# Turning results back twelve products after their last one, also across the border of batches

## The chip, the cores and the metric

The kernel runs on one core of one Trainium2 chip. The metric is device time in microseconds (us) of one execution; the figures given are the median of a few runs. TensorE (PE in the profile) multiplies and transposes, VectorE (DVE) and ScalarE (ACT) work on tiles and read the matmul results, GpSimd (POOL) works on tiles in main on-chip memory, and SyncE (SP) issues most of the transfers. Each engine has a queue of its own and runs it in the order in which the program lists the work; they meet through semaphores.

## The reference

For 8 batches, 8 heads, a sequence of 576 and a head size of 64, attention that keeps the 32 largest scores of each row, then a low-rank mixer over the sequence and a two-layer network over the channels:

```python
scores = scale * np.matmul(q, k.transpose(0, 1, 3, 2))
kth = np.partition(scores, -top_k, axis=-1)[..., -top_k:-top_k + 1]
scores = np.where(scores >= kth, scores, -1000000000.0)
attn = softmax(scores)                     # with + 1e-09 in the denominator
x = heads_to_channels(np.matmul(attn, v))  # (8, 576, 512)
xt = x.transpose(0, 2, 1)
u = x + (xt @ U @ V).transpose(0, 2, 1)    # rank 32
ch = np.maximum(u @ w_ch1, 0.0) @ w_ch2    # 512 -> 2048 -> 512
return (u + ch).astype(np.float32)
```

## The kernel before

Attention runs in 160 steps: 32 pairs of heads (four pairs to a batch), five row tiles to a pair. The main loop (from L788) lists, for each step, work on several tiles at once: score products for the next tile (`scores`, L323) with ScalarE copies out of PSUM (L351, L340), the search for the 32nd largest value on VectorE and GpSimd (`fold`, `split`, `front`), exponentials on ScalarE (L397), and the turning of the weights so that they can be multiplied with V. In the later pairs most of that turning is shared: VectorE transposes 32 x 32 blocks (`blocks`, L518), SyncE writes them to a scratch tensor in DRAM (L524), and ScalarE issues the transfer that brings them back as PT (`back`, L533); a last strip is transposed by TensorE (`turns`, L557) and copied by ScalarE (L558). `values` multiplies PT with V (L587, L591; L577 for the fifth tile). When a pair is done, `mixed` turns its result (L614, L618), divides by the sums of the weights on GpSimd (L619), and makes the pair's part of u, transposed (L625, L633, L637, L639, L647).

The two-layer network of a batch is `mlp(b)`, a generator of single products. It is put on the list `fillers` when the batch's last pair is mixed, and `fill()`, called some nine times in a step, draws products from it by a running balance `due`, so that they are spread between the attention work on TensorE's queue. The 576 columns of u are done in two parts, 320 and 256 wide. For each part there are 16 blocks of the hidden layer, of four products each (L662) and a Relu on ScalarE (L674), and then four blocks of results, c = 0 to 3, of sixteen products each (L681). A block of results is copied from PSUM by ScalarE (L696), and GpSimd adds u (L697); in the last batch VectorE does both in one (L694). The matmul results lie in two PSUM buffers (`ps_m`, two deep), and the hidden layer in ten pairs of tiles.

The result tile oT is still transposed. The function `turned_back` makes a job for it: TensorE transposes it in two or three pieces (L729) into a PSUM buffer of `ps_t`, two deep and shared with `turns`, `values` and `mixed`; ScalarE copies it to ob (L731, and L733 for the last 64 rows, which belong to the first part); SyncE writes it out (L735, L740). In the last batch the job is a VectorE transpose (L711) with transfers from it (L716, L721), but for its very last result. The job isn't run at once, but kept in the list `late`:

```python
if f == 4 and late:        # after the Relu of hidden block 4: 20 products on
    late.pop()()
...
if f == 12 and late:       # in the next block of results: 13 products on
    late.pop()()
...
late.append(turned_back(b, chunks, lo, c, oT))
...
late.pop()()               # end of mlp(b): the last result of the batch, at once
```

So the results c = 0, 1, 2 are turned back after 13 more products, the result c = 3 of the first part after 20, and the last one of the batch directly after its own addition.

Of the kernel before, what the change touches and what calls it, by code (L numbers as in the profile page):

```python
# [26 lines left out]
def kernel(  # L27
# [98 lines left out]
    def rows(t):  # L126
        return P if t < NT else TAIL
# [475 lines left out]
    def mixed(g, wait, lag=0):  # L603
# [45 lines left out]
        if gi == NPAIR - 1:  # L649
            fillers.append(mlp(b))  # L650

    def mlp(b):

        uT = uTs.pop(b)
        late = []
        for chunks, (lo, hi) in zip(PARTS, SPAN):
            w = hi - lo
            hTs = []
            for f in range(NF):
                ph = ps_m.tile([P, C], F32, tag="mm", name="mm")  # L660
                for cc in range(NC):
                    nc.tensor.matmul(  # L662
                        ph[:, 0:w],
                        lhsT=w1[:, cc, f * P : (f + 1) * P],
                        rhs=uT[:, cc, lo:hi],
                        start=(cc == 0),
                        stop=(cc == NC - 1),
                    )
                    if cc < NC - 1:
                        yield w / C  # L670
                if f % 2 == 0:
                    hT = mlpp.tile([P, 2, WIDE], F32, tag="hT", name="hT", bufs=HT)
                    hTs += [hT[:, 0], hT[:, 1]]
                nc.scalar.activation(hTs[f][:, 0:w], ph[:, 0:w], AF.Relu)  # L674
                if f == 4 and late:
                    late.pop()()
                yield w / C
            for c in range(NC):
                po = ps_m.tile([P, C], F32, tag="mm", name="mm")
                for f in range(NF):  # L680
                    nc.tensor.matmul(  # L681
                        po[:, 0:w],
                        lhsT=w2[:, f, c * P : (c + 1) * P],
                        rhs=hTs[f][:, 0:w],
                        start=(f == 0),
                        stop=(f == NF - 1),
                    )
                    if f == 12 and late:
                        late.pop()()
                    if f < NF - 1:  # L690
                        yield w / C
                oT = mlpp.tile([P, WIDE], F32, tag="oT", name="oT")
                if b == B - 1:
                    nc.vector.tensor_tensor(oT[:, 0:w], uT[:, c, lo:hi], po[:, 0:w], ALU.add)  # L694
                else:
                    nc.scalar.copy(oT[:, 0:w], po[:, 0:w])  # L696
                    nc.gpsimd.tensor_tensor(oT[:, 0:w], oT[:, 0:w], uT[:, c, lo:hi], ALU.add)  # L697
                late.append(turned_back(b, chunks, lo, c, oT))
                yield w / C
        late.pop()()  # L700

    def turned_back(b, chunks, lo, c, oT):


        def run():
            cs = slice(c * P, (c + 1) * P)
            if b == B - 1 and (lo, c) != (SPAN[1][0], NC - 1):

                w = sum(rows(t) for t in chunks)
                ob = mlpp.tile([P, 3 * P], F32, tag="ob", name="ob", bufs=2)  # L710
                nc.vector.transpose(ob[:, 0:w], oT[:, 0:w])  # L711
                for a in range(4):
                    cs = slice(c * P + a * BLK, c * P + (a + 1) * BLK)
                    ba = ob[a * BLK : (a + 1) * BLK]
                    for t in chunks[0:2]:
                        nc.sync.dma_start(  # L716
                            out[b, 0:MAIN, cs].rearrange("(m i t) c -> t i m c", i=BLK, t=NT)[t],
                            ba[:, OFF[t] - lo : OFF[t] - lo + P].rearrange("i (m c) -> i m c", c=BLK),
                        )
                    if NT in chunks:  # L720
                        nc.sync.dma_start(  # L721
                            out[b, MAIN:S, cs].rearrange("(m i) c -> i m c", i=BLK),
                            ba[:, 2 * P : 2 * P + TAIL].rearrange("i (m c) -> i m c", c=BLK),
                        )
                return
            tp = ps_t.tile([P, 3, P], F32, tag="tp", name="tp")
            for i, t in enumerate(chunks):
                n = rows(t)
                nc.tensor.transpose(tp[0:n, i, :], oT[:, OFF[t] - lo : OFF[t] - lo + n], ident)  # L729
            ob = mlpp.tile([P, 3, P], F32, tag="ob", name="ob", bufs=2)  # L730
            nc.scalar.copy(ob[:, 0:2], tp[:, 0:2, :])  # L731
            if NT in chunks:
                nc.scalar.copy(ob[0:TAIL, 2], tp[0:TAIL, 2, :])  # L733
            t = chunks[0]
            nc.sync.dma_start(  # L735
                out[b, 0:MAIN, cs].rearrange("(p t) c -> p t c", t=NT)[:, t : t + 2, :],
                ob[:, 0:2],
            )
            if NT in chunks:
                nc.sync.dma_start(out[b, MAIN:S, cs], ob[0:TAIL, 2])  # L740

        return run
# [11 lines left out]
    def fill(k=1):  # L754


        nonlocal due
        for _ in range(k):
            if passes:
                passes.pop(0)()  # L760
            if mixing and next(mixing[0], True):
                mixing.pop(0)
            due += share * (SHORT if t == NT else 1) * (EARLY if n <= 2 * ALONE + 2 else 1)
            while due > 0:
                if not fillers:
                    due = 0.0
                    break
                done = next(fillers[0], None)
                if done is None:
                    fillers.pop(0)  # L770
                else:
                    due -= done
# [132 lines left out]
        fill(2)  # L905
    while mixing or fillers:
        fill()


# [29 lines left out]
```

## Time and profile before

| what | value |
|---|---|
| median of 3 runs | 1717.11 us (1716.77 to 1718.14) |
| profiled execution, own time | 1716.93 us |
| its span, first to last instruction | 1715.1 us |
| TensorE matmul busy | 1612.5 us (94%) |
| VectorE busy | 1485.3 us (87%) |
| ScalarE busy | 1023.3 us (60%) |
| GpSimd busy | 944.3 us (55%) |
| mean granted TensorE clock | 0.970 |

In the profile, a line such as "L729 PE MATMUL" is work of line 729 of the kernel on TensorE; "out<-in" names the tile that is written and those that are read. "PE x <- POOL y" in a list of waits means that TensorE stood before x until GpSimd had done y. PEld is TensorE's loading of weights, which overlaps its matmuls. A product in float32 shows as two matmul records. Ends of matmuls are modelled, and some records may be missing. The attention ends at about 1555 us, and from about 1587 us on only the last batch's network is left, 128 us long. Batches 2 to 5 repeat with a period of 193.8 us.

### The profile page before, as it was taken

The page shows a single profiled execution, that of the slowest core. Times are in us where ns is not written, and L with a number is a line of the kernel's source. Part 1 is how long each engine was busy: PE and PEld are TensorE (multiplying, and loading weights), DVE is VectorE, ACT ScalarE, POOL GpSimd, SP SyncE. Part 2 cuts the span into 40 slices and gives each one's busy share as a digit, 9 for nine tenths or more (in the row PEclk, how much of TensorE's full clock was granted, in tenths as well). Part 3 has the DMA queues.
Part 4 walks back from the last instruction along what each step waited for, and adds up shares of the span by engine and source line. Part 5 has one row for each costly group of instructions (what it writes and reads, how often), then busy time and mean ns, then how long its engine had stood idle before and what let it go on. Part 6 is the DMA issues. An engine that isn't in the chain of part 4 may idle for free.

```text
span 1715.1 us, 29634 instructions
## 1 busy us (share of the span) xinstructions
PE 1612.5 (94%) x9489; PEld 1218.3 (71%) x9489; DVE 1485.3 (87%) x4317; ACT 1023.3 (60%) x2582; POOL 944.3 (55%) x749
## 2 busy tenths in 40 slices
PE   4566799998999999999999999999999999999999
PEld 2444566787777877788677877788677877788777
DVE  7999989999999999999999999999999999992000
ACT  4888797665656556565656566565655566563100
POOL 4778578656555555565555555565555555552000
PEclk7678899999999999999999999999999999999999
DMA  3322322344444444444444444444444444432010
GB/s 86 95 84 84 84 75 62 79 113 124 117 112 118 115 112 106 116 112 118 111 112 115 115 110 107 115 105 122 112 111 119 116 109 102 114 93 71 4 16 13
DMA packets 275837, 167.37 MB, mean 98 GB/s; under 512 B 173920, under 2 KB 260192, under 8 KB 275680
## 3 DMA queue, kind: packets, MB, share of 16 engines
q1 hardware_dynamic: 259648, 110.67, 27.5%
q10 hardware_dynamic: 16032, 54.79, 9.9%
q8 instruction: 75, 1.23, 0.3%
q14 instruction: 82, 0.67, 0.1%
HBM read 101.42 MB, written 63.96 MB: 96 GB/s over the span
## 4 chain that ended last, share of the span: by engine, by line
PE 68%; DVE 25%; DMA 2%; issue 2%; POOL 2%; ACT 1%; SPq 1%; DVEq 0%; POOLq 0%; ACTq 0%
PE mm L662 25%; PE mm L681 21%; DVE upper L458 8%; DVE m L463 7%; PE sc L323 7%; PE O L591 5%; DVE first L446 3%; DVE y L518 1%; PE tp L557 1%; PE O L577 1%; PE up L637 1%; PE O L587 1%; DVE lower L434 1%; DVE upper L436 1%; DVE upper L432 1%
## 5 line engine op out<-in xcount | busy, mean ns | idle before, releaser
L681 PE MATMUL mm<-hT,w 128*128 128x256 f32 (+1 forms) x2048 | 531.2, 408 | 0.0
L662 PE MATMUL mm<-uT,w 128*128 128x256 f32 (+1 forms) x2048 | 522.9, 407 | 0.7 <-ACT hT L674 0.7
L491 POOL TENSOR_TENSOR Ssb<-Ssb,E 128x576 f32<-128x576 f32 x271 | 379.1, 1417 | 245.5 <-ACT E L488 245.2
L662 PEld LDWEIGHTS mm<-uT,w 128*128 128x128 f32 x2048 | 379.9, 191 | 98.5 <-issue 2.6
L681 PEld LDWEIGHTS mm<-hT,w 128*128 128x128 f32 x2048 | 378.8, 192 | 93.7 <-issue 4.2
L463 DVE MAX8 m<-upper 128x8 f32<-128x304 f32 (+1 forms) x864 | 408.0, 509 | 3.6
L458 DVE MATCH_REPLACE8 upper<-m,upper 128x304 f32<-128x304 f32 (+1 forms) x576 | 285.9, 503 | 0.0
L390 POOL TENSOR_TENSOR lower<-Ssb 128x576 uint32<-128x576 uint32 (+1 forms) x135 | 174.2, 1290 | 145.8 <-ACT Ssb L351 45.3
L393 POOL TENSOR_TENSOR lower<-lower,upper 128x576 uint32<-128x576 uint32 (+1 forms) x135 | 173.8, 1288 | 111.8 <-DVE upper L392 104.2
L397 ACT ACTIVATE Ssb<-Ssb,nmax 128x576 f32<-128x576 f32 x286 | 221.3, 776 | 19.5 <-POOL Ssb L468 10.2
L674 ACT ACTIVATE hT<-mm 128x320 f32<-128x320 f32 (+1 forms) x256 | 104.9, 410 | 192.7 <-PE mm L662 186.7
L323 PE MATMUL sc<-qkT 64*128 64x288 f32 x1334 | 209.7, 436 | 9.0 <-ACT Ssb L358 8.0
L488 ACT ACTIVATE E<-Ssb,least 128x576 f32<-128x576 f32 x271 | 198.0, 769 | 5.2
L323 PEld LDWEIGHTS sc<-qkT 64*128 64x128 f32 x1334 | 115.1, 182 | 64.0 <-issue 24.1
L351 ACT COPY Ssb<-sc 128x576 f32<-128x576 f32 x216 | 127.5, 642 | 33.4 <-PE sc L323 31.7
L518 DVE STREAM_TRANSPOSE y<-Ssb 128x512 f32<-128x512 f32 x208 | 134.7, 683 | 14.4 <-ACT Ssb L397 14.3
L591 PE MATMUL O<-PT,va 128*64 128x128 f32 x2048 | 143.9, 284 | 2.3 <-DMA PT<-away 2.3
L694 DVE TENSOR_TENSOR oT<-uT,mm 128x320 f32<-128x320 f32 (+1 forms) x8 | 3.6, 455 | 144.0 <-PE mm L681 144.0
L591 PEld LDWEIGHTS O<-PT,va 128*64 128x64 f32 x2048 | 112.7, 140 | 18.9 <-DMA PT<-away 3.0
L432 DVE MAX8 upper<-lower 128x8 f32<-128x288 f32 x243 | 98.0, 439 | 22.6 <-POOL lower L393 20.9
L458 DVE MATCH_REPLACE8 upper<-first,upper 128x304 f32<-128x304 f32 x243 | 110.0, 459 | 0.0
L392 DVE TENSOR_TENSOR upper<-sc,Ssb 128x576 f32<-128x576 f32 (+1 forms) x135 | 92.2, 683 | 20.3 <-ACT Ssb L351 19.7
(91 smaller groups left out, 1878.7 us busy)
## 6 DMA issues: line engine op xcount, KB each, us to landing
away<-y SPq DMA_DIRECT2D x416, 128.0 KB, 2.4
PT<-away ACTq DMA_DIRECT2D x104, 512.0 KB, 3.3
raw<-in_moe_w_ch_dram SPq DMA_DIRECT2D x32, 512.0 KB, 3.8
va<-in_v_dram SPq DMA_DIRECT2D x64, 128.0 KB, 2.3
out_dram<-ob SPq DMA_DIRECT2D x57, 128.0 KB, 2.0
ld<-in_q_dram SPq DMA_DIRECT2D x108, 64.0 KB, 3.0
ld<-in_k_dram SPq DMA_DIRECT2D x108, 64.0 KB, 2.4
ld<-in_q_dram SPq DMA_DIRECT2D x108, 8.0 KB, 3.2
```

Source lines behind the costliest of these rows:

```text
L323: nc.tensor.matmul(out, lhsT=qkT[half(h), 0, cols(t)], rhs=qkT[half(h), 1, lo:hi], start=True, stop=True,)
L390: nc.gpsimd.tensor_tensor(bottom, a.bitcast(U32), b.bitcast(U32), ALU.add)
L393: nc.gpsimd.tensor_tensor(bottom, bottom, top.bitcast(U32), ALU.subtract)
L397: nc.scalar.activation(E, chunk, AF.Exp, bias=nmax, scale=SCALE, accum_out=total)
L458: nc.vector.match_replace(nxt, ms[c], curs[c], NEG)
L463: nc.vector.max(ms[c], curs[c])
L488: nc.scalar.activation(gap, chunks[c], AF.Relu, bias=least[:, c : c + 1], scale=-WIDEN)
L491: nc.gpsimd.tensor_tensor(chunks[c], chunks[c], gap, ALU.subtract)
L518: nc.vector.transpose(y[:, :, h].rearrange("p r c j -> p c r j"), E2[:, a : a + MAIN].rearrange("p (c r j) -> p c r j", c=NT, r=4),)
L591: nc.tensor.matmul(O[half(h)], lhsT=va[:, h, j, :], rhs=PB[:, h, j] if shared(g, t) else PT[:, NT * h + j], start=False, stop=(j == NT - 1),)
L662: nc.tensor.matmul(ph[:, 0:w], lhsT=w1[:, cc, f * P : (f + 1) * P], rhs=uT[:, cc, lo:hi], start=(cc == 0), stop=(cc == NC - 1),)
L681: nc.tensor.matmul(po[:, 0:w], lhsT=w2[:, f, c * P : (c + 1) * P], rhs=hTs[f][:, 0:w], start=(f == 0), stop=(f == NF - 1),)
```

## The change

The list `late` and its three places go. Instead a count of products, `ticks`, runs through all batches; a job is booked for a count of twelve more, and each product of either layer calls `tick()`, which runs the first booked job when its count has come. The end of a batch runs nothing any more: its last job falls due in the next batch's network. After the main loop, what is still booked is run off.

```diff
+    posts, ticks = [], 0
+
+    def later(wait, job):
+        posts.append((ticks + wait, job))
+
+    def tick():
+        nonlocal ticks
+        ticks += 1
+        if posts and posts[0][0] <= ticks:
+            posts.pop(0)[1]()
+
     def mlp(b):
         uT = uTs.pop(b)
-        late = []
...
                         stop=(cc == NC - 1),
                     )
+                    tick()
                     if cc < NC - 1:
                         yield w / C
...
                 nc.scalar.activation(hTs[f][:, 0:w], ph[:, 0:w], AF.Relu)
-                if f == 4 and late:
-                    late.pop()()
                 yield w / C
...
                         stop=(f == NF - 1),
                     )
-                    if f == 12 and late:
-                        late.pop()()
+                    tick()
                     if f < NF - 1:
                         yield w / C
...
-                late.append(turned_back(b, chunks, lo, c, oT))
+                later(12, turned_back(b, chunks, lo, c, oT))
                 yield w / C
-        late.pop()()
...
     while mixing or fillers:
         fill()
+    while posts:
+        tick()
```

The tick comes directly after the product and ahead of the Relu of its block, so a job that falls due with the fourth product of a hidden block is listed before that Relu. The twelfth product after a result c = 3 is the fourth of hidden block f = 2.

## The prediction

> **What bounds the kernel now.** I read the page's totals and slices first. The rows are busy time and share, then busy tenths in 40 slices of the span.
>
> ```profile
> PE 1612.5 (94%) x9489; PEld 1218.3 (71%) x9489; DVE 1485.3 (87%) x4317; ACT 1023.3 (60%) x2582; POOL 944.3 (55%) x749
> ...
> PE   4566799998999999999999999999999999999999
> ...
> DVE  7999989999999999999999999999999999992000
> ```
>
> TensorE and VectorE both look full until about 1580 us, so the totals alone don't say which one sets the pace. The list of waits does. First TensorE's waits between 428 and 1580 us, then those between 420 and 428 us, then VectorE's in one batch period, 1207 to 1400 us (total, times, longest):
>
> ```profile
> PE tp L729 <- POOL oT L697: 6.3, 5, 1.3
> PE O L591 <- DMA PT<-away: 0.2, 1, 0.2
> ...
> PE tp L729 <- POOL oT L697: 2.1, 1, 2.1
> PE up L637 <- ACT Tb L633: 0.9, 1, 0.9
> ...
> DVE upper L392 <- ACT Ssb L351: 3.4, 3, 1.7
> DVE y L518 <- ACT Ssb L397: 2.8, 1, 2.8
> DVE upper L432 <- POOL lower L393: 1.8, 2, 1.3
> ```
>
> In 1152 us TensorE waits six times, five of them on one line: the transposes of a batch's last result wait for GpSimd's addition. VectorE waits 8.0 us per period of 193.8 us, mostly on ScalarE copies of score products, so it follows TensorE. One such border, in order of time (start, duration, idle in brackets):
>
> ```profile
> 1204.17 0.60 PE L681 MATMUL mm<-hT,w 128*128 128x256 f32 x2
> ...
> 1205.25 0.73 POOL L697 TENSOR_TENSOR oT<-oT,uT 128x256 f32<-128x256 f32 x1 [0.21 <-DVE upper L458]
> ...
> 1206.04 0.44 PE L729 MATMUL tp<-ident,oT 128*128 128x128 f32 x2 [1.27 <-POOL oT L697]
> 1206.31 6.09 PE L662 MATMUL mm<-uT,w 128*128 128x320 f32 x22
> ```
>
> The last product ends at 1204.77, ScalarE copies it, GpSimd adds until 1205.98, and TensorE stands for 1.27 us although the next batch's products, which need nothing of this, are already behind it in its queue.
>
> **What the Trainium skill says.** "Perfetto Trace Analysis", section "Identifying the Most-Contended Engine", warns that TensorE's busy share is a poor measure of its limit, as pipelined matmuls overlap. So I checked the rate: in the tail, where TensorE is alone, 128 records of L662 take 34.45 us in the chain, 269 ns each; in the steady part 22 records take 5.92 us, the same 269 ns. It is really saturated. "TensorE: Matmul & The Clock Gate", section "Step-by-step: what each phase is for", says that matmuls stay in program order, and its "Architectural detail" section that ScalarE is strictly first in, first out; the trace agrees (the 1.27 us above; ScalarE waits 14.5 us in six ob copies per period). The clock gate is used below.
>
> **The change part by part.** Each product is two matmul records (2048 of L662 for 8 x 2 x 16 x 4 = 1024 products).
>
> *The border jobs of batches 0 to 6 move 12 products on.* Removed waits: five of 1.27 us (624.7, 818.5, 1012.3, 1206.0 and 1399.8), one of 1.32 us at 1586.4, one of 2.13 us at 423.5. The two transposes cost some 0.22 us in the stream of matmuls in either place, so they cancel.
>
> Five steady borders: 5 x 1.27 = 6.35 us. Does the rest keep up? VectorE's 2.82 us wait at 1209.9 hangs on an exp that stands on ScalarE behind the Relu of the next batch's first product, so it moves with TensorE, and so do the score copies at 1214.4. What is new is the landing place. These are TensorE's and ScalarE's timelines there:
>
> ```profile
> 1214.74 0.33 PE L557 MATMUL tp<-ident,Ssb 128*128 128x128 f32 x1
> 1214.91 4.47 PE L662 MATMUL mm<-uT,w 128*128 128x320 f32 x16
> ...
> 1219.53 1.09 PE L591 MATMUL O<-PT,va 128*64 128x128 f32 x16
> ...
> 1215.44 0.28 ACT L558 COPY PT<-tp 128x128 f32<-128x128 f32 x1
> 1215.65 0.44 ACT L674 ACTIVATE hT<-mm 128x320 f32<-128x320 f32 x1
> 1215.79 0.33 ACTq L533 DMA_DIRECT2D PT<-away  x1
> ```
>
> Eleven products run before this point (22 records), so the twelfth is the first after L557, and the transposes start at about 1214.91 + 0.54 = 1215.45. The ob copy (0.37 us) can run 0.42 us later, at 1215.87, and stands ahead of the Relu of f=2, which starts at about 1216.14 in place of 1215.65, and ahead of the PT transfer that ScalarE issues: 0.49 us late. The transfer lands 3.2 us after its issue, at 1219.0 now, and L591 needs it at 1219.53: 0.53 us of slack, plus 0.22 us because TensorE carries the transposes here: 0.75 against 0.49. That leaves 0.26 us for the output transfer, now issued by SyncE at about 1216.3 beside the PT transfer. No row shows just these two together; its bounds are 0 and the slowest PT flight in the trace, 5.3 us, 2.1 more. I take 0.1 us lost per batch start, since a PT flight at 1398.7, with an output issue beside it, took 3.4. That is 5 x 0.1 = 0.5.
>
> Behind the ob copy also stand the two exps at 1215.98 and 1216.74, awaited by VectorE's y at 1217.2: about 0.25 us late against TensorE's 0.22, so level. The product with f=4 needs the Relu of f=2 after 0.22 + 4 x 0.54 = 2.4 us; it ends by 1.2. SyncE stands idle from about 1212 to 1218.5 and then issues the next away transfer, so a 0.39 us issue at 1216.3 delays nothing. GpSimd's queue gets and loses nothing.
>
> *Batch 6's border*: after 1580 VectorE has no attention work, TensorE runs alone: the full 1.32 us.
>
> *Batch 0's border*: removing 2.13 us does more and less than that.
>
> ```profile
> 421.80:425.20 3.40, 0.99 (x12) 0.56 (x12) 3.40 (x13) 1.34 (x6) 2.32 (x3) 1.00 0.21 83
> 425.20:428.60 3.40, 3.24 (x14) 2.51 (x16) 3.40 (x11) 2.06 (x5) 2.17 (x3) 0.50 0.29 73
> ```
>
> Columns: stretch, then busy time of TensorE, its loads, VectorE, ScalarE, GpSimd, the granted clock (third from the end). After a stretch with 0.99 of 3.40 us busy the clock was halved for 3.4 us. The skill's clock page, "What's actually happening", states such a window of about 3.4 us; the trace agrees. So TensorE may get here 1.6 us (pT at 422.8, when L619 is done, then up without L633's queue) and 1.7 us of clock. But VectorE has no wait at all from 428 to 487 us: it paces here. The product at 444.46 needs a PT transfer issued at 441.00, which needs an away transfer issued at 436.73 to 438.04 and landed 2.4 us later, at 440.4. It can be issued 0.6 us earlier, and has 0.36 us of slack at its other end: the gain is cut at 0.95, less a little margin: 0.8 us. Bounds: 0 and 3.3.
>
> *The other 42 results of batches 0 to 6* go one product, 0.43 or 0.54 us, earlier, and the 7 at the border of halves 8 products earlier. Cost nothing: ScalarE comes early to these copies and waits; the closest buffer, at 1281.3, is freed at 1279.87 and would be needed at 1280.8. If this cover went, it would be some 0.5 us each. At the half border the Relu of f=2 now stands behind two copies (0.37 + 0.26); it ends about 1.3 us after its product, needed after 2.05. The loads of the next pair (1316 to 1331) stay ahead of those two output transfers on SyncE.
>
> *The last batch*: seven VectorE transposes, where that engine waits 144 us in total anyway: nothing. Its last job still follows its addition at once: the tail from 1711.0 stays.
>
> Sum: 6.35 - 0.5 + 1.32 + 0.8 = 8.0 us. The profiled execution took 1716.93 with a span of 1715.1, so the span becomes 1707.1 and the execution 1708.9; the median, 1717.11, is 0.2 above: **1709.1 us**.
>
> **Rivals.** *Everything comes back, the clock too*: 6.35 + 1.32 + 3.05 (both waits at 420 to 428) = 10.7, so 1706.4. For it: TensorE has no other wait. Against: VectorE's unbroken run to 487.
>
> *The wait moves to the PT transfer*: if the output transfer beside it adds 1.0 us (flight 4.2, seen beside loads), L591 waits 0.74 rather than 0.1 in six batches: 3.9 lost, 1713.0. For it: 0.53 is the tightest such slack. Against: at 1398.7 the two met and 0.2 was lost.
>
> *Slower*: the same place, but the two transfers halve each other's rate: flight 6.4, L591 waits 3.2 + 0.49 - 0.75 = 2.9 us in six batches, 17.6 us against 8.5 gained: about 1726. It decides from a delay of 1.4 us more than the slack per batch. Against: no PT flight in the trace was over 5.3.
>
> *No difference*: VectorE's chain is the true bound, and the 1.27 us only comes to stand elsewhere: 1717. For it: 184 of 194 us busy. Against: its waits are on TensorE's products.
>
> **How the numbers follow.** Mine 0.60, with its own range 1707.5 to 1711; everything back 0.13; wait at the transfer 0.12; no difference 0.07; slower 0.08. From everything back to the moved wait is 0.85, so the range is 1705.5 to 1713.6. A measurement of this kernel can tell about 0.2% (3.4 us): faster 0.84, same 0.08, slower 0.08.
>
> **What would show it.** Right: no TensorE wait on L697 before 1700 us, a period of 192.6 in place of 193.8 us, VectorE's wait near the border about 1.3 us shorter relative to the old time. A TensorE wait on PT some 13 us after each border shows the transfer rival; an unchanged period with VectorE waits gone shows the bound by VectorE. I'd be wrong by most if shifts in ScalarE's order made transposes or score products wait in places with less than 1 us of slack.

## The result

| | before | after |
|---|---|---|
| median | 1717.16 us (4 runs, 1716.77 to 1718.14) | 1706.30 us (4 runs, 1705.57 to 1707.34) |
| profiled execution, own time | 1716.93 us | 1705.85 us |
| its span | 1715.1 us | 1704.0 us |

After over before is 0.9935, with a 95% interval of 0.9922 to 0.9947: 10.9 us less, where 8.0 had been forecast. A second series with the same kernel gave 0.9933 (0.9917 to 0.9950).

In the profile after, the line numbers below the change have moved: L662 became L674 (first layer), L674 became L687 (Relu), L681 became L692 (second layer), L697 became L707 (GpSimd's addition), L729 became L737 (the transposes), L731 became L739 (ScalarE's copy to ob). First the page's totals of after:

```profile
PE 1611.5 (95%) x9489; PEld 1218.9 (72%) x9489; DVE 1484.2 (87%) x4317; ACT 1020.7 (60%) x2582; POOL 944.9 (55%) x749
```

The work is the same, with 9489 matmul records in 1611.5 us against 1612.5, so what went is idle time. TensorE's waits after, from 426 to 1548 us, are down to one, and that is early in batch 1:

```profile
PE O L591 <- DMA PT<-away: 0.5, 1, 0.5
```

From 1196 to 1388 us TensorE is busy for 192.00 of 192.00 us. The border of a batch, in order of time, now reads like this on TensorE:

```profile
1197.62 0.60 PE L692 MATMUL mm<-hT,w 128*128 128x256 f32 x2
1198.05 6.08 PE L674 MATMUL mm<-uT,w 128*128 128x320 f32 x22
...
1206.48 0.33 PE L557 MATMUL tp<-ident,Ssb 128*128 128x128 f32 x1
1206.65 0.70 PE L674 MATMUL mm<-uT,w 128*128 128x320 f32 x2
1207.19 0.38 PE L737 MATMUL tp<-ident,oT 128*128 128x128 f32 x2
1207.40 3.93 PE L674 MATMUL mm<-uT,w 128*128 128x320 f32 x14
```

The last product of the old batch starts at 1197.62 and the first of the new one 0.43 us later, where 2.14 us lay between them before (1204.17 to 1206.31). The two transposes come after the twelfth product and take a place of 0.21 us in the stream (1207.19 to 1207.40). Before, from the last product to the next batch's first, 2.14 us held 0.43 us of product and these 0.21 to 0.22 us of transposes. So 1.49 us were lost there, more than the 1.27 us that the list of waits had.

That number can be checked closely, because batches 2 to 5 repeat: the distance between the same ScalarE copy (L600) in successive batches was 193.76 us before, with one value of 193.80, and is 192.27 us after in each of four periods. The difference is 1.49 us per batch.

VectorE's waits from 1200 to 1392 us after:

```profile
DVE upper L392 <- ACT Ssb L351: 4.1, 4, 1.7
DVE upper L432 <- POOL lower L393: 1.3, 2, 0.8
DVE y L518 <- ACT Ssb L397: 1.1, 1, 1.1
```

They sum to 6.5 us in place of 8.0. The wait on the exp at the border fell from 2.8 to 1.1 us, and the rest is still mostly a wait for score copies: VectorE follows TensorE, with less slack.

The two profiles differ by 11.1 us of span, and one stretch of that can't come from the change: the 17th L600 copy comes at 234.2 us before and at 232.7 after, and no result is turned back before 293 us in either. The ten other profiles of this study have it between 232.4 and 234.2, whatever was changed. They fall into two groups, at 232.4 to 232.7 and at 233.7 to 234.2. The variants with the border at one and at eight products list the same work up to there and lie in different groups; but a second profile of each kernel fell into the group of its first (234.0 and 232.7). What puts an execution into one group or the other stays open. So single spans are good to about 1.5 us, and the study goes by stretches and periods where it can.

### The profile page after: what moved, and what is told of

The parts are those of the page before. It is cut to its first block, busy times and chain, and to the rows that moved or that the text cites. A ratio compares the mean times of both kernels' runs of the same rounds, so it can differ in the third digit from the quotient of the medians.

```text
span 1704.0 us, 29640 instructions
## 1 busy us (share of the span) xinstructions
PE 1611.5 (95%) x9489; PEld 1218.9 (72%) x9489; DVE 1484.2 (87%) x4317; ACT 1020.7 (60%) x2582; POOL 944.9 (55%) x749
## 4 chain that ended last, share of the span: by engine, by line
PE 79%; DVE 13%; ACT 3%; POOL 2%; DMA 2%; issue 1%; SPq 0%; DVEq 0%; POOLq 0%; ACTq 0%
PE mm L674 27%; PE mm L692 26%; PE sc L323 9%; PE O L591 6%; DVE upper L458 4%; DVE m L463 4%; PE O L577 2%; PE tp L557 2%; PE up L637 2%; DVE first L446 1%; PE O L587 1%; PE tp L552 1%; PE up L639 1%; PE pT L625 1%; DMA PT<-away 1%
## 5 line engine op out<-in xcount | busy, mean ns | idle before, releaser
L692 PE MATMUL mm<-hT,w 128*128 128x256 f32 (+1 forms) x2048 | 532.0, 408 | 0.0
L674 PE MATMUL mm<-uT,w 128*128 128x256 f32 (+1 forms) x2048 | 525.1, 408 | 0.0
L674 PEld LDWEIGHTS mm<-uT,w 128*128 128x128 f32 x2048 | 380.1, 191 | 97.3 <-issue 2.9
L692 PEld LDWEIGHTS mm<-hT,w 128*128 128x128 f32 x2048 | 378.4, 192 | 93.2 <-issue 3.9
L687 ACT ACTIVATE hT<-mm 128x320 f32<-128x320 f32 (+1 forms) x256 | 104.9, 410 | 178.4 <-PE mm L674 172.5
L591 PE MATMUL O<-PT,va 128*64 128x128 f32 x2048 | 143.2, 283 | 3.3 <-DMA PT<-away 3.2
L591 PEld LDWEIGHTS O<-PT,va 128*64 128x64 f32 x2048 | 112.1, 139 | 19.9 <-DMA PT<-away 4.3
```

The costliest lines, as they stand in the source:

```text
L591: nc.tensor.matmul(O[half(h)], lhsT=va[:, h, j, :], rhs=PB[:, h, j] if shared(g, t) else PT[:, NT * h + j], start=False, stop=(j == NT - 1),)
L674: nc.tensor.matmul(ph[:, 0:w], lhsT=w1[:, cc, f * P : (f + 1) * P], rhs=uT[:, cc, lo:hi], start=(cc == 0), stop=(cc == NC - 1),)
L692: nc.tensor.matmul(po[:, 0:w], lhsT=w2[:, f, c * P : (c + 1) * P], rhs=hTs[f][:, 0:w], start=(f == 0), stop=(f == NF - 1),)
```

## The experiments

**Without the border.** The change inside batches alone; the last result of a batch goes at once, as before:

```diff
                 later(12, turned_back(b, chunks, lo, c, oT))
                 yield w / C
+        while posts:
+            posts.pop(0)[1]()
```

> The change without its border part: results inside a batch are turned back after twelve products, the last one of a batch at once, as before. Border theory (all the gain is at the seven borders between batches, the other 49 moved results cost and bring nothing): 1717 us, within 1 us of before, period of batches 2 to 5 193.8 us, five TensorE waits of 1.27 us on the addition. Rival (the 1.5 us per period that the changed kernel shows are 1.27 us from the border and 0.22 us from the other moved results): period 193.55 us and about 1715 us.

Measured: 1717.73 us against 1716.80 us of the kernel before in the same series, ratio 1.0003 (0.9995 to 1.0012), period 193.76 us in every batch. Its TensorE waits between 450 and 1560 us are the old ones:

```profile
PE tp L740 <- POOL oT L707: 6.4, 5, 1.3
```

The results that move within their batch, 49 of them in batches 0 to 6, bring nothing and cost nothing.

**The border alone**, in the kernel before:

```diff
-        late.pop()()
+        later(12, late.pop())
```

with `tick()` after each product and the run-off at the end as in the change.

> The kernel before, with the last result of each batch alone moved twelve products into the next batch; the others stay at thirteen and twenty. Border theory: the whole gain, 1706 to 1707 us, period 192.3 us, no TensorE wait on the addition before the last batch's end. Rival (a part comes from the other moved results): period 192.5 us, 1708 us.

Measured: 1708.12 us, ratio 0.9948 (0.9932 to 0.9965), period 192.27 us, no TensorE wait from 450 to 1550 us. The period is exactly that of the full change. The time is not: it lies some 2 us above that of the changed kernel in its two series, where the rival had put it. In the profile, 1.1 us of it lie in the stretch before 234 us that no result is turned back in, and 1.3 us in one TensorE wait on PT at 1553.7, where the changed kernel has 0.12. SyncE issues nothing there from 1547.2 to 1557.8 us, so no moved result's transfer runs beside that PT transfer, which took 4.5 us; whether the other results' places or chance made it long was not tested further.

**Two products, one product.** The distance of the border's job, with all others at twelve:

```diff
-                later(12, turned_back(b, chunks, lo, c, oT))
+                later(2 if lo and c == NC - 1 else 12, turned_back(b, chunks, lo, c, oT))
```

> The changed kernel, but the last result of a batch is turned back two products into the next batch in place of twelve. Stream theory (what a border costs is the spacing from the last product to the next batch's first product, 2.14 us, less the 0.43 and 0.22 us that the product and two transposes take in a stream: 1.49 us, of which 1.44 is waiting): two products of 0.54 us hide 1.08 us, 0.36 to 0.41 us stay, period 192.3 + 0.4 = 192.7 us. Listed-wait theory (the wait is 1.27 us as listed): 0.19 us stay, period 192.5 us.

> The changed kernel, but the last result of a batch is turned back one product into the next batch. Stream theory: one product of 0.54 us hides 0.54 of the 1.44 us, and a wait adds a little for restarting the stream: 0.90 to 0.95 us stay, period 193.2 us, although the list of waits will show only 0.7 us of it. Listed-wait theory: 0.73 us stay, period 193.0 us.

Measured, in one run each: 1707.62 us and periods of 192.68 us with two products, 1710.62 us and 193.22 us with one. TensorE's waits from 450 to 1560 us, with two products first, then with one:

```profile
PE tp L737 <- POOL oT L707: 1.0, 5, 0.2
```

```profile
PE tp L737 <- POOL oT L707: 3.7, 5, 0.7
```

| distance in products | listed wait, us | lost per period, us (period less 192.27) | difference, us |
|---|---|---|---|
| 0 (before) | 1.27 | 1.49 | 0.22 |
| 1 | 0.73 | 0.95 | 0.22 |
| 2 | 0.19 | 0.41 | 0.22 |
| 8, 12 | none | 0 | |

The stream theory named 0.36 to 0.41 us for two products and 0.90 to 0.95 us for one, the other theory 0.19 and 0.73. Each product of 0.54 us hides 0.54 us of the wait, and a listed wait costs 0.22 us more than it says. Batch 6's border, which has no attention work behind it, agrees: 1.32 us were listed there, and the stretch from the last L600 copy to the end got 1.54 us shorter. By this line three products would have been enough, at 1.27 + 0.22 = 1.49 us or 2.8 products; that distance itself was not run.

**Eight products**: the same edit with 8.

> The changed kernel, but the last result of a batch is turned back eight products into the next batch, in the middle of a run of eleven, away from the PT transfer. Period 192.27 us as with twelve, the PT transfer lands 0.5 us or more ahead of its product in place of 0.07 to 0.31, its flight is 3.2 us in place of 3.4 to 3.7. Time as the changed kernel, 1705.5 to 1707 us. If room at that transfer cost time, it would be up to 0.3 us per batch faster.

Measured: 1706.81 us, ratio 0.9941 (0.9924 to 0.9958), period 192.27 us. The PT transfer lands 0.52 to 0.61 us ahead of the L591 that reads it, after flights of 3.1 to 3.2 us. In the changed kernel these are 0.07 to 0.31 us, and 3.4 to 3.7. So the landing place does narrow the room at that transfer, and the narrowing costs nothing.

**The copy three times**, to see where that room ends:

```diff
-            nc.scalar.copy(ob[:, 0:2], tp[:, 0:2, :])
+            for _ in range(3 if lo and c == NC - 1 and b < B - 1 else 1):
+                nc.scalar.copy(ob[:, 0:2], tp[:, 0:2, :])
```

> The changed kernel, in which ScalarE makes the copy of a batch's last result three times in place of once, so that the PT transfer behind it goes out some 0.6 to 0.7 us later. In the changed kernel that transfer lands 0.07 to 0.31 us ahead of the product that reads it. Landing theory (this place has no more room than that): TensorE waits 0.3 to 0.6 us on PT once in each batch, period 192.6 to 192.9 us. Rival (the room is larger, or the loss is taken up by other engines): period 192.27 us, no such wait.

Measured: 1709.96 us in one run, periods of 192.84 to 193.05 us. TensorE's waits from 450 to 1548 us:

```profile
PE O L591 <- DMA PT<-away: 3.0, 5, 0.7
```

Five waits of 0.50 to 0.66 us, one per batch, on the transfer that was named. With two more copies of 0.37 us that transfer goes out 0.81 us later and the period grows by 0.6 to 0.8 us: most of the delay is lost, somewhat more than was expected. The changed kernel stands within 0.3 us of that edge.

**Batch 0 at once**: the changed kernel, with batch 0's border as before.

```diff
                 later(12, turned_back(b, chunks, lo, c, oT))
                 yield w / C
+        while posts and b == 0:
+            posts.pop(0)[1]()
```

> The changed kernel, but the last result of batch 0 is turned back at once, the other borders stay moved. My step (VectorE paces batch 1, so batch 0's border is worth 0.8 us): 0.8 us slower than the changed kernel, some 1707.1 us. Everything-back rival (both waits there and the halved clock come back in full): 3 us slower, some 1709.3 us. If it brought nothing and the start of the kernel merely varies from run to run: 1706.3 us. The period stays 192.3 us in each case.

Measured: 1708.90 us, ratio 0.9952 (0.9938 to 0.9967), period 192.27 us: 2.6 us above the changed kernel's 1706.30, though that is from another series. The border alone, of the same series, took 1708.12, only 0.8 us less, or 2.0 us if its longer wait at 1553.7 is taken off. So the times alone don't say whether the rival or my 0.8 was nearer. The premise of my step can be looked at, in VectorE's waits from 428 to 487 us:

```profile
DVE upper L392 <- ACT Ssb L351: 0.9, 1, 0.9
```

My cap rested on VectorE having no wait at all in this stretch. Here it has one.

**The kernel before once more**, and **the changed kernel once more**, without edits, for second profiles.

> The kernel before once more, for a second profile. I took batch 0's border to be capped by VectorE, which had no wait from 428 to 487 us in the profile of before. The variants with that border at once show VectorE waits of 1.2 us at 435 to 442 us. If the first profile was an odd execution at that place: VectorE waits of about 1.2 us there in this profile too, and 291.6 us from the 17th to the 41st pair-tile of values rather than 290.2. If the variants differ by their moved results: no VectorE wait there again.

> The changed kernel once more, beside the others of this series. 1706 to 1707 us, period 192.27 us. Its profile shows how much the first 234 us, where no result is turned back yet, differ between executions: they took 234.2 us before and 232.7 after; if that was chance, this one may lie anywhere between.

Measured: 1718.05 us in one run for before; 1705.90 us for after, ratio 0.9933 (0.9917 to 0.9950), period 192.27 us. VectorE's waits from 428 to 487 us in the second profile of before:

```profile
DVE upper L392 <- ACT Ssb L351: 0.9, 1, 0.9
DVE y L518 <- ACT Ssb L397: 0.2, 1, 0.2
```

So the same kernel does wait there in another execution. The stretch from the 17th to the 41st L600 copy holds batch 0's border and none of the other six:

| batch 0's last result | profiles | us from the 17th to the 41st copy |
|---|---|---|
| at once | before | 290.2 |
| at once | before again, without the border, batch 0 at once | 291.8, 291.6, 291.9 |
| twelve products on | after, after again, the border alone | 289.6, 290.3, 289.3 |
| twelve products on | the copy three times, the slower pace (below) | 289.5, 289.3 |
| eight, two, one product on | three variants | 289.4, 289.1, 289.0 |

Of the four profiles with that border at once the first stands apart, by 1.5 us. Against the other three, batch 0's border is worth about 2.1 us (291.7 less 289.7 for twelve and eight products); against the first profile alone it would be 0.5.

**A slower pace in the early pairs**, to fill the rest of batch 0's gap. In the changed kernel TensorE's waits from 420 to 445 us are, beside the one of 0.5 us on PT that is shown above,

```profile
PE pT L625 <- POOL x L619: 1.9, 1, 1.9
...
PE up L637 <- ACT Tb L633: 0.4, 1, 0.4
```

because batch 0's products run out before batch 1's are ready. With a slower pace they last:

```diff
-    SLOTS, SHORT, EARLY = 8, 0.65, 0.91
+    SLOTS, SHORT, EARLY = 8, 0.65, 0.87
```

> The changed kernel with the pace of the network in the early pairs at 0.87 in place of 0.91, so that batch 0's products last until batch 1's are ready; otherwise TensorE stands for 1.9 and 0.35 us at batch 0's border and 0.5 us after it. If TensorE's idle time there is lost time: up to 2.7 us faster than the changed kernel, 1704 us. If VectorE's chain sets the pace up to there: no difference, 1706.3 us. Period 192.27 us in both cases.

Measured: 1706.84 us, ratio 0.9941 (0.9926 to 0.9955): not faster than the changed kernel (0.9933 in the same series). The waits at the border are gone, and TensorE's list from 405 to 520 us has this one alone:

```profile
PE O L591 <- DMA PT<-away: 0.9, 1, 0.9
```

A part of the time saved stands a little later at the transfer, and the stretch of the table above is no shorter than in other variants, at 289.3 us. Here the chain from VectorE through the scratch tensor does set a limit, at the product that I had named; only the gain up to it is larger than my 0.95 us if the three profiles are taken, not the first. No variant of the study was faster than the change.

## Why the prediction was right, and where its sizes were wrong

The direction and the mechanism held: all the gain is at the seven borders, TensorE is the bound, VectorE follows it, and the moved results inside batches are free. The size was too small. The time lies below the 1707.5 to 1711 us that stood beside the likeliest case, at the 1706.4 us of the rival in which everything comes back. That rival hit by luck: it had 6.35 us for the steady borders, where 7.45 were measured, and 3.05 us for batch 0's, the clock with it, where about 2.1 were. These are the terms of the sum:

| term | forecast, us | measured, us | from |
|---|---|---|---|
| five steady borders, wait removed | 6.35 | 7.45 | period, 5 x 1.49 |
| their landing place | -0.5 | 0 | period with eight products the same as with twelve |
| batch 6's border | 1.32 | 1.54 | stretch from the last L600 copy to the end: 152.68 to 151.14 |
| batch 0's border | 0.8 | about 2.1 (0.5 by the first two profiles) | stretches above |
| sum | 8.0 | about 11.1 | medians: 10.9 and 11.5 in two series |

That the sum meets the medians is weaker support than it looks. In the two pairs of profiles, before with after and the two taken again, the terms of the steady borders and of batch 6 come to 9.1 and 8.9 us. Batch 0's stretch gives 0.5 and 1.5 us, and the stretch before it, in which nothing was changed, gives 1.5 and 1.3 us. The steady borders and batch 6's are firm; how the last 2 us are shared between batch 0's border and that early stretch isn't.

*Steady borders.* The step that failed took the listed idle time as the price of a wait. A wait is counted from the end of the matmul before, 1204.77 here, but in a full stream the next one would have started 0.43 us after that product's start, at 1204.60. The 0.17 us between are the tail of a matmul that otherwise overlaps with its successor, and the restart of the stream took another 0.05 (0.27 in place of 0.22 us for the transposes). I had used 0.22 us for the transposes as cancelling between the two places, and had the spacing of starts in front of me: 2.14 less 0.65. The runs with one and two products show the same 0.22 us at each size of the wait.

*The landing place.* The forecast had the PT transfer issued 0.49 us late and lost 0.1 us per batch. ScalarE's timeline after:

```profile
1207.61 0.37 ACT L739 COPY ob<-tp 128x256 f32<-128x256 f32 x1
1207.75 0.33 ACTq L533 DMA_DIRECT2D PT<-away  x1
1207.88 0.44 ACT L687 ACTIVATE hT<-mm 128x320 f32<-128x320 f32 x1
```

L533 goes out 1.27 us after the start of L557 (1206.48 to 1207.75), where it was 1.05 before (1214.74 to 1215.79): 0.22 us late, not 0.49, since it doesn't wait for the copy and the Relu to be done. It goes out before the Relu that precedes it in program order has even started. So the strict order of ScalarE's queue, on which the forecast leaned, did not hold here for the issue of a transfer; the sentence ahead of the forecast that each engine runs its work in the order listed needs that exception. In exchange its flight grew by 0.2 to 0.5 us beside the output transfer, more than the 0.1 I took. The flight at 1398.7 that I had taken that from had its output transfer issued 1.97 us behind it (1400.67), here it is 0.25 us. The two errors went against each other, by luck: 0.07 to 0.31 us of room was left, and nothing was lost. The place was rightly named as the tightest: the run with three copies shows TensorE waiting just there.

*Batch 0's border.* This step failed in its premise. "VectorE has no wait at all from 428 to 487 us" was true of one execution. Three other profiles with that border as before have VectorE waits of 0.9 to 1.2 us at 435 to 442 us, so in those VectorE did not pace up to there. The cap itself is in the runs, and at the product I had named. With this border moved, TensorE waits there on PT in seven of eight profiles, for 0.2 to 1.7 us; with it at once, in none of four. The changed kernel has 0.5 us at 442.4 and none in its second profile. The border alone shows it best; of its TensorE waits from 426 to 450 us the longest is

```profile
PE O L591 <- DMA PT<-away: 1.5, 1, 1.5
```

In it the last of the four away transfers lands at 439.77, the PT transfer goes out at 439.87 and lands at 443.20, and L591 starts at 443.25, so the chain that I had described sets the time there.

I had also counted on the clock, and the profiles show little or nothing of it. With the border moved, five profiles have no halved stretch between 415 and 435 us (after, the border alone, one product, the copy three times, the slower pace); those with eight and two products have one of 3.4 us, the second profile of after one of 6.8 us. From the 17th to the 41st copy the five take 289.0 to 289.6 us, the two 289.4 and 289.1, and the last 290.3. Where the clock is full, TensorE stands at PT the longer: 0.5 to 1.7 us, against 0.2 and 0.3 beside 3.4 us of halved clock.

*Signs named beforehand.* No TensorE wait on the addition before 1700 us: so. A period of 192.6: it was 192.27. The VectorE wait near the border some 1.3 us shorter: 1.7 (2.8 to 1.1). A TensorE wait on PT some 13 us after each border, the sign of the transfer rival: none after batches 1 to 5. The two rivals without a gain have nothing for them in the runs.

## What to carry to other kernels

Price a wait of TensorE by the spacing of starts across it, less what the work between takes in a full stream, and not by the listed idle time; where the stream repeats, the period tells the price to a hundredth of a microsecond, better than the run time does. A job whose input takes two more engines should be listed a few products behind them, also across the end of a loop; here eight were enough, and two hid all but 0.41 us. And before a cap is built on "this engine never waits here", see whether a second profile of the same kernel says so too.

## What the runs showed of the hardware

- A listed TensorE wait of 1.27, 0.73 or 0.19 us in a stream of float32 matmuls costs 1.49, 0.95 or 0.41 us: 0.22 us more each time.
- ScalarE issues a transfer while instructions ahead of it in program order still stand in its queue: L533 at 1207.75, the Relu listed ahead of it from 1207.88.
- Behind the five steady borders the 512 KB PT transfer takes 3.1 to 3.2 us with the result turned back eight products on, and 3.4 to 3.7 us with twelve, where a 128 KB output transfer is issued some 0.25 us after it.
- Profiles of kernels that list the same work up to there reach the 17th L600 copy at 232.4 to 234.2 us, and the stretches in which TensorE's clock is halved differ from profile to profile.
- In the two variants with 3.4 us of halved clock just behind batch 0's border the stretch around it was no longer than in those without (289.4 and 289.1 us, against 289.0 to 289.6), and TensorE waited less at the PT transfer that follows (0.3 and 0.2 us, against 0.5 to 1.7).
